# A single-core decode block: the last 256 rows of w2 by one indirect load of Pool's, and twelve rows to a partition

## The chip, the cores and the metric

The kernel runs on one core of one Trainium2 chip, and the core's five engines run side by side, each through its own list of instructions: TensorE (PE, with its weight loads shown as PEld), VectorE (DVE), ScalarE (ACT), GpSimd (POOL) and SyncE (SP), which here only issues transfers. Sixteen DMA engines carry out the transfers that SP, ACT and POOL issue.

The metric is the device time of one launch in microseconds (us). Before the change it is 391.63 us, the median of three runs (391.55 to 391.79). One more execution was recorded by the profiler; its own time is 391.81 us, and its recorded span, from the first instruction to the last, is 390.0 us.

## The reference

One decode step of a transformer block for 8 sequences, one token each, width D = 512. A condition vector gives six modulation vectors. Attention has 32 query heads and 8 key/value heads of width 128 over the last W = 2048 positions of a cache. A dense layer with F = 1792 hidden units and a squared ReLU follows.

```python
mod = (_silu(c) @ w_mod).reshape(8, 6, 1, -1)
sa, ca, ga, sb, cb, gb = (mod[:, i] for i in range(6))
h = _layernorm(x) * (1 + ca) + sa
q = (h @ wq).reshape(B, 1, 32, 128).transpose(0, 2, 1, 3)
k, v = (jnp.repeat(t[:, :, Sk - W:, :], 4, axis=1) for t in (k_cache, v_cache))
p = _softmax(jnp.einsum("bhqd,bhkd->bhqk", q, k) * 128 ** -0.5)
x = x + ga * (merge(jnp.einsum("bhqk,bhkd->bhqd", p, v)) @ wo)
h = _layernorm(x) * (1 + cb) + sb
r = jnp.maximum(h @ w1 + b1, 0)
x = x + gb * ((r * r) @ w2 + b2)
```

All of it is in float32. Nearly all the bytes are the cache: 8 sequences times 16.8 MB of K and V, beside w_mod (6.3 MB), wq and wo (8.4 MB each), w1 and w2 (3.7 MB each).

## The kernel before, in words

**Staging.** Four buffers of 4 MB, `slots`, hold whatever was loaded from DRAM. The list `loads` has the order: w_mod in two halves, wq in two halves, then for each sequence b two K loads and two V loads of 4 MB (the V loads one sequence behind), then wo in two halves, w1 and w2. `pump` issues the next loads on SP's queue as long as a slot is free, and `done` gives a slot back and calls `pump`. So a load can be issued only when the work on an earlier slot's content is over. The instruction list is written out by hand in this order; no scheduler moves anything.

**Completion semaphores.** A transfer of SP's or ACT's signals its landing on one of eight semaphores (DMAHW0 to DMAHW7 in the instruction lists). They are dealt out in rotation, in the order in which the transfers of both queues stand in the program. A transfer that is dealt a semaphore for the second time waits, in its issuing engine's list, until the earlier transfer on that semaphore has landed. Transfers that POOL issues have semaphores of their own (DMASW).

**Start.** Before the first `pump()` the program issues the small inputs: four transfers of `xc` (the token and condition rows) and `b1_in` on ACT (L63, L67), `b1_x` and `b2_in` on POOL (L68, L69). Then DVE and ACT make the SiLU of c, PE multiplies with w_mod (L238), DVE normalises, and PE multiplies with wq (L260).

**Each sequence.** DVE transposes K in place, in 32 by 32 blocks (`turn`, L307), PE multiplies with the queries (`scores`, L317), DVE and ACT make the softmax, and PE multiplies with V (`weighted`, L400) and collects the heads (`gather`).

**The dense layer, which the change rewrites.** w2 has 1792 rows, 14 to each of 128 partitions. Thirteen to a partition (FC = 13) come in five pieces into the last slot (L109 to L114): 4, 4, 3, 1 and 1 rows. The remaining 128 rows (`EXTRA`) go, four to a partition, to 20 and 12 partitions of `w2x`, which is the memory of `qb_all` used again; the two transfers stand on SP's queue behind w1 and ahead of the pieces of w2 (L106 to L108). POOL has zeroed the 64 partitions before (L325). The hidden units of the thirteen rows are computed by L517 and L520 in `ph`, those of the last 128 by L527 and L529 in `px`. ACT takes the ReLU of both (L542, L545), and DVE squares and transposes them (L551 to L555). The product with w2 runs in two parts. The first four rows of a partition and `w2x` go through a 512-wide accumulator (L562), which DVE and ACT copy out (L566, L567) and four matmuls fold in (L579). All other rows, 4 to 12, are multiplied by L572 straight into `py`, in the order in which their pieces land. L585, L586 and the store L587 end the program.

Of the kernel before, what the change touches and what calls it, by code (L numbers as in the profile page):

```python
# [18 lines left out]
def tile_adaln_cached_attention_mlp(  # L19
# [24 lines left out]
    FC = F // P - 1  # L44
# [19 lines left out]
    b1_in = consts.tile([NQ, FG], F32, name="b1_in")  # L64
# [3 lines left out]
    nc.gpsimd.dma_start(b1_x, b1[P * FC :].rearrange("(g n) -> g n", g=1))  # L68
# [12 lines left out]
    def load(key):  # L81
# [121 lines left out]
    rep = consts.tile([P, 4, 4, 32], F32, name="rep")  # L203
# [20 lines left out]
    rx = consts.tile([64, 32, 4], F32, name="rx")  # L224
# [84 lines left out]
    def scores(b, t):  # L309
# [14 lines left out]
        if b == B - 1 and t == 1:  # L324
            nc.gpsimd.memset(w2x[:64, :], 0.0)  # L325
# [184 lines left out]
    h2d = work.tile([P, NQ, 2, 32], F32, name="h2d", tag="prd", bufs=4)  # L510
    nc.vector.tensor_copy(h2d, h2T[:, :, None, :].to_broadcast([P, NQ, 2, 32]))
# [15 lines left out]
    nc.tensor.matmul(px[:64, :FX], one[:1, :1].to_broadcast([1, 64]), b1_x, start=True, stop=False)  # L527
    for kc in range(NQ):
        nc.tensor.matmul(  # L529
            px[:64, :FX],  # L530
            h2d[:, kc].rearrange("p a b -> p (a b)"),
            w1t[:, kc, P * FC :],
            start=False,
            stop=(kc == NQ - 1),
        )
    r = work.tile([P, 32, FC], F32, name="relu", tag="a")
    rT = work.tile([P, FC, 32], F32, name="rT", bufs=1)
    rxT = work.tile([64, 4, 32], F32, name="rxT", bufs=1)
    h = ph[:, :FG].rearrange("p (l c) -> p l c", l=32)
    halves = ((0, 6), (6, FC))  # L540
    for lo, hi in halves:
        nc.scalar.activation(r[:, :, lo:hi], h[:, :, lo:hi], AF.Relu)  # L542

    for g, o, _, at_ in EXTRA:
        nc.scalar.activation(  # L545
            rx[g : g + 32, : 4 * o, :].rearrange("p (o i) c -> p i o c", i=4),
            px[g : g + 32, at_ : at_ + 16 * o].rearrange("p (i o c) -> p i o c", i=4, o=o),
            AF.Relu,
        )
    for lo, hi in halves:  # L550
        nc.vector.tensor_mul(r[:, :, lo:hi], r[:, :, lo:hi], r[:, :, lo:hi])  # L551
        nc.vector.transpose(rT[:, lo:hi], r[:, :, lo:hi].rearrange("p l c -> p c l"))
        if lo == 0:
            nc.vector.tensor_mul(rx, rx, rx)
            nc.vector.transpose(rxT, rx.rearrange("p l c -> p c l"))  # L555

# [3 lines left out]
    chunks += [(rxT[:, c, :], w2x[:64, D * c : D * c + D]) for c in range(4)]  # L560
# [63 lines left out]
```

## Time and profile before

| | |
|---|---|
| median of three runs | 391.63 us |
| the profiled execution: its own time, its span | 391.81 us, 390.0 us |
| PE busy | 257.2 us, 66% of the span |
| DVE busy | 215.7 us, 55% |
| ACT, POOL busy | 42.8 us and 6.6 us |
| moved by DMA | 165.05 MB, mean 423 GB/s |
| on SP's queue | 7096 packets, 164.70 MB, 98.4% of the 16 DMA engines' time |
| mean granted TensorE clock | 0.836 of full speed |

The profile's page gives busy time by engine, the span in 40 slices, the chain of work that ended last, and the costliest groups of instructions. A timeline row has the start in us, the duration in us, the engine, the source line (L114 is line 114), the operation, the tile written and the tiles read, the shapes, a count, and in brackets the idle time of the engine ahead of it with what ended it. A name that ends in "q" (SPq) is the engine's sequencer. PE, PEld, DVE and ACT rows that follow each other are merged, so "x8" is eight records; a float32 matmul shows as two records. In the rows by window the last three numbers are the granted TensorE clock, the mean busy share of the 16 DMA engines and GB/s; packets are counted whole where they start.

### The profile page before, as it was taken

What the parts mean: (1) busy time and instruction counts of PE and PEld (TensorE: products, weight loads), DVE (VectorE), ACT (ScalarE), POOL (GpSimd) and SP (SyncE); (2) the same over time, 40 slices, a digit from 0 to 9 for tenths busy, and PEclk for the clock granted to TensorE, in tenths of its full rate; (3) what the DMA queues carried; (4) which work ended last, traced back from release to release, by engine and by line L of the source; (5) the groups of instructions that cost most, each with busy time, mean ns of one, the idle gap of its engine ahead of it and who ended that gap; (6) DMA issues with size and microseconds to landing.
All of it is one profiled execution on the core that took longest, in us unless ns stands there. A gap on an engine that the chain in (4) does not pass through costs nothing.

```text
span 390.0 us, 4820 instructions
## 1 busy us (share of the span) xinstructions
PE 257.2 (66%) x2126; PEld 111.1 (28%) x2126; DVE 215.7 (55%) x234; ACT 42.8 (11%) x91; POOL 6.6 (2%) x14
## 2 busy tenths in 40 slices
PE   0272808678975694859485938394749475985975
PEld 0120201151351343124322422233223313452332
DVE  3420199399394939293928391939292938330032
ACT  0310100030030003000300020003000300032010
POOL 4000000000000000000000000000000000100000
PEclk9998758969975986889778987797688779888889
DMA  8999999999999999999999999999999999999995
GB/s 325 432 434 428 430 430 434 434 444 439 435 437 428 427 432 434 430 428 430 429 430 428 434 430 432 437 439 430 439 434 434 426 437 425 434 435 413 424 421 207
DMA packets 7253, 165.05 MB, mean 423 GB/s; under 512 B 888, under 2 KB 1056, under 8 KB 1696
## 3 DMA queue, kind: packets, MB, share of 16 engines
q1 hardware_dynamic: 7096, 164.70, 98.4%
q8 instruction: 17, 0.28, 0.3%
q10 hardware_dynamic: 72, 0.04, 0.0%
q14 instruction: 4, 0.03, 0.0%
q0 software_dynamic: 64, 0.00, 0.0%
HBM read 164.67 MB, written 0.07 MB: 422 GB/s over the span
## 4 chain that ended last, share of the span: by engine, by line
DMA 53%; DVE 25%; PE 20%; ACT 1%; issue 1%; DVEq 0%; ACTq 0%; SPq 0%
DMA slot<-in_A_k_cache_dram 34%; DVE slot L307 22%; PE s_ps L317 16%; DMA slot<-in_B_w_dram 9%; DMA slot<-in_A_wq_dram 7%; DMA slot<-in_w_mod_dram 3%; PE t_ps L260 2%; PE t_ps L388 1%; PE o_ps L400 1%; PE m_ps L276 1%; DVE pT L389 0%; ACT prd L378 0%; DVE s L331 0%; DVE s L335 0%; DVE mx L340 0%
## 5 line engine op out<-in xcount | busy, mean ns | idle before, releaser
L307 DVE STREAM_TRANSPOSE slot<-slot 128x2048 f32<-128x2048 f32 x64 | 143.9, 2284 | 41.7 <-DMA slot<-in_A_k_cache_dram 41.7
L317 PE MATMUL s_ps<-slot,qb_all 128*32 128x512 f32 x512 | 121.7, 1099 | 68.4 <-DVE slot L307 67.5
L317 PEld LDWEIGHTS s_ps<-slot,qb_all 128*32 128x32 f32 x512 | 22.3, 136 | 147.7 <-issue 82.1
L400 PE MATMUL o_ps<-slot,pT 128*32 128x256 f32 x1024 | 59.7, 382 | 0.0
L400 PEld LDWEIGHTS o_ps<-slot,pT 128*32 128x32 f32 x1024 | 46.0, 112 | 27.7 <-issue 18.8
L388 PE MATMUL t_ps<-ident,prd 128*128 128x128 f32 x128 | 27.1, 373 | 16.5 <-ACT prd L378 9.5
L331 DVE STREAM_TRANSPOSE s<-s_ps 128x512 f32<-128x512 f32 x8 | 5.7, 717 | 54.2 <-PE s_ps L317 54.2
L388 PEld LDWEIGHTS t_ps<-ident,prd 128*128 128x128 f32 x128 | 20.2, 189 | 22.3 <-ACT prd L378 21.8
L378 ACT ACTIVATE prd<-pr,rz 128x512 f32<-128x512 f32 x32 | 20.5, 710 | 9.4 <-DVE rz L370 9.4
L354 ACT ACTIVATE pr<-s,nm 128x512 f32<-128x512 f32 x8 | 5.8, 722 | 141.2 <-DVE nm L348 141.2
L389 DVE TENSOR_TENSOR pT<-t_ps,m 128x512 f32<-128x512 f32 x32 | 20.4, 670 | 1.3 <-PE t_ps L388 1.2
L410 ACT COPY o_sb<-o_ps 128x256 f32<-128x256 f32 x16 | 5.8, 363 | 122.1 <-PE o_ps L400 122.1
L260 PE MATMUL t_ps<-slot,h1T 128*32 128x512 f32 x64 | 9.8, 764 | 8.9 <-DMA slot<-in_A_wq_dram 6.9
L475 PE MATMUL s_ps<-slot,oT 128*32 128x512 f32 x56 | 8.5, 773 | 4.5 <-DMA slot<-in_A_wo_dram 4.5
L173 PE MATMUL m_ps<-xsum,sel 128*128 128x1 f32 x2 | 0.6, 362 | 16.5 <-DVE xsum L196 16.5
L294 DVE TENSOR_TENSOR qb_all<-qrep,block 128x512 f32<-128x512 f32 x8 | 9.0, 1124 | 3.0 <-ACT qrep L286 3.0
L272 DVE STREAM_TRANSPOSE qT<-t_ps 128x512 f32<-128x512 f32 x2 | 1.4, 717 | 15.9 <-PE t_ps L260 15.7
L366 PE MATMUL m_ps<-z,same 128*128 128x1 f32 x16 | 3.3, 273 | 9.5 <-ACT pr L354 9.5
L238 PE MATMUL m_ps<-slot,cT 128*32 128x384 f32 x64 | 7.8, 658 | 0.0
L325 POOL MEMSET qb_all<- 64x2048 f32 x1 | 1.8, 1807 | 331.9 <-PE s_ps L317 331.9
L489 DVE COPY at_i<-s_ps 128x256 f32<-128x256 f32 x1 | 0.4, 425 | 12.2 <-PE s_ps L475 12.2
L260 PEld LDWEIGHTS t_ps<-slot,h1T 128*32 128x32 f32 x64 | 2.4, 133 | 16.1 <-DMA slot<-in_A_wq_dram 7.8
(113 smaller groups left out, 102.5 us busy)
## 6 DMA issues: line engine op xcount, KB each, us to landing
slot<-in_A_k_cache_dram SPq DMA_DIRECT2D x16, 4096.0 KB, 18.6
slot<-in_A_v_cache_dram SPq DMA_DIRECT2D x16, 4096.0 KB, 28.2
slot<-in_A_wq_dram SPq DMA_DIRECT2D x2, 4096.0 KB, 26.4
slot<-in_w_mod_dram SPq DMA_DIRECT2D x2, 3072.0 KB, 17.2
slot<-in_A_wo_dram SPq DMA_DIRECT2D x1, 4096.0 KB
slot<-in_A_wo_dram SPq DMA_DIRECT2D x1, 2048.0 KB
slot<-in_A_wo_dram SPq DMA_DIRECT2D x2, 1024.0 KB
slot<-in_B_w_dram SPq DMA_DIRECT2D x2, 1024.0 KB
```

What stands on the lines that cost most here:

```text
L238: nc.tensor.matmul(pm[i][32 * q : 32 * q + 32, : 3 * P].rearrange("p (m n) -> p m n", m=3), cT[:, kc, :], wm[:, 3 * i : 3 * i + 3, q, :], ...
L260: nc.tensor.matmul(pq[t][32 * x : 32 * x + 32, :], hT[:, kc, :], w[:, 2048 * t + 512 * x : 2048 * t + 512 * x + 512], start=(kc == 0), sto ...
L294: nc.vector.tensor_mul(qb[b % 2][:, :, :, :REP], qrep_b[:, :, None, :, b].to_broadcast([P, 32, 4, REP]), block[:, None, :, None].to_broadc ...
L307: nc.vector.transpose(k, k)
L317: nc.tensor.matmul(S_[b][32 * x : 32 * x + 32, :].rearrange("p (j i) -> p j i", i=8), q[:, n : n + 32], k[:, :, c, :, x], start=(t == 0 an ...
L354: nc.scalar.activation(pr.rearrange("p j (a i) -> p j a i", a=4), S2_.pop(b).rearrange("p (a j i) -> p j a i", a=4, i=8), AF.Exp, bias=NM_ ...
L378: nc.scalar.activation(d, pr[:, 4 * n : 4 * n + 4, :, None].to_broadcast([P, 4, 32, 4]), AF.Copy, scale=RZ_[b][0])
L388: nc.tensor.transpose(pp[:, P * i : P * i + P], d[:, i].rearrange("p i u -> p (i u)"), one)
L389: nc.vector.tensor_mul(PT_[b][:, n].rearrange("p q j (x r) -> p q (j x) r", r=REP), pp.rearrange("p (y q r) -> p q y r", y=16, r=REP), m16 ...
L400: nc.tensor.matmul(o[32 * (m % 4) : 32 * (m % 4) + 32].rearrange("p u d -> p (u d)"), PT_[b][:, n, 2 * q + t, 2 * u : 2 * u + 2, :].rearra ...
L410: nc.scalar.copy(O_[b][:, t], o)
L475: nc.tensor.matmul(wo_ps[32 * (i % 4) : 32 * (i % 4) + 32, :], oT[:, i, :], slot(("wo", i // 16), D)[:, i % 16, :], start=(i < 4), stop=(i ...
```

## The change

FC becomes 12: twelve rows of w2 to a partition come by SP's queue, in pieces of 4, 4, 2, 1 and 1 rows. The last 256 rows, in 64 groups of four (8 KB), go to 64 of the 128 partitions of `w2x` by one indirect load of POOL's, L348. It reads a list of 128 group numbers, one for each partition; a number beyond the last group means that nothing is moved to this partition. `EXTRA` now lists the chosen partitions as (quarter, first lane, number of lanes, first group): all of partitions 0 to 20, 27 to 44, 48 to 51, 60 to 68, 92 to 99 and 124 to 127. The list is made at the start, by a memset and nine iotas on POOL (L233, L235), a transpose and a conversion on DVE (L243, L245). The load is issued behind the memset of `w2x` (now all 128 partitions), after the last scores. `b1_x` and `b2_in` move from POOL's queue to ACT's. The hidden units of the last rows are now 256: `px` is computed for 128 columns of output partitions and 256 values wide, its ReLU is split into four pieces on ACT and five on DVE, and DVE handles `rx` behind the second half of `r` rather than ahead of it.

```diff
-    FC = F // P - 1
+    FC = F // P - 2
...
-    nc.gpsimd.dma_start(b1_x, b1[P * FC :].rearrange("(g n) -> g n", g=1))
-    nc.gpsimd.dma_start(b2_in, b2.rearrange("(g n) -> g n", g=NQ))
-    EXTRA = ((0, 5, P * FC, 0), (32, 3, P * FC + 80, 80))
+    nc.scalar.dma_start(b1_x, b1[P * FC :].rearrange("(g n) -> g n", g=1))
+    nc.scalar.dma_start(b2_in, b2.rearrange("(g n) -> g n", g=NQ))
+    EXTRA = (
+        (0, 0, 21, 0), (0, 27, 5, 21), (1, 0, 13, 26), (1, 16, 4, 39), (1, 28, 4, 43),
+        (2, 0, 5, 47), (2, 28, 4, 52), (3, 0, 4, 56), (3, 28, 4, 60),
+    )
...
-            for g, o, first, _ in EXTRA:
-                v = w2[first : first + 16 * o].rearrange("(i o c) n -> o i (c n)", i=4, o=o)
-                nc.sync.dma_start(w2x[g : g + 4 * o, :], v)
-            cuts = ((0, 4), (4, 8), (8, 11), (11, 12), (12, 13))
+            cuts = ((0, 4), (4, 8), (8, 10), (10, 11), (11, 12))
...
+    place_r = work.tile([P, 32], F32, name="mt", bufs=1)
+    nc.gpsimd.memset(place_r, float(F))
+    for g, l, n, first in EXTRA:
+        nc.gpsimd.iota(place_r[32 * g : 32 * g + 1, l : l + n], pattern=[[1, n]],
+            base=P * FC // 4 + first, channel_multiplier=0, allow_small_or_imprecise_dtypes=True)
+    place_c = work.tile([P, 32], F32, name="nm")
+    nc.vector.transpose(place_c, place_r)
+    nc.vector.tensor_copy(places, place_c[:, 0:1])
...
-            nc.gpsimd.memset(w2x[:64, :], 0.0)
+            nc.gpsimd.memset(w2x, 0.0)
+            nc.gpsimd.indirect_dma_start(w2x, None, w2.rearrange("(r c) n -> r (c n)", c=4),
+                bass.IndirectOffsetOnAxis(ap=places[:, :1], axis=0),
+                bounds_check=F // 4 - 1, oob_is_err=False)
...
-    nc.tensor.matmul(px[:64, :FX], one[:1, :1].to_broadcast([1, 64]), b1_x, start=True, stop=False)
+    nc.tensor.matmul(px[:, :FX], one[:1, :1].to_broadcast([1, P]), b1_x, start=True, stop=False)
...
-    for g, o, _, at_ in EXTRA:
-        nc.scalar.activation(
-            rx[g : g + 32, : 4 * o, :].rearrange("p (o i) c -> p i o c", i=4),
-            px[g : g + 32, at_ : at_ + 16 * o].rearrange("p (i o c) -> p i o c", i=4, o=o), AF.Relu)
-    for lo, hi in halves:
+    for i, (g, l, n, first) in enumerate(EXTRA):
+        to = rx[32 * g : 32 * g + 32, l : l + n, :]
+        v = px[32 * g : 32 * g + 32, 4 * first : 4 * (first + n)].rearrange("p (l c) -> p l c", c=4)
+        if i % 2:
+            nc.scalar.activation(to, v, AF.Relu)
+        else:
+            late.append((to, v))
+    for n, (lo, hi) in enumerate(halves):
+        if n:
+            for to, v in late:
+                nc.vector.tensor_scalar(to, v, 0.0, None, op0=ALU.max)
         nc.vector.tensor_mul(r[:, :, lo:hi], r[:, :, lo:hi], r[:, :, lo:hi])
-        nc.vector.transpose(rT[:, lo:hi], r[:, :, lo:hi].rearrange("p l c -> p c l"))
-        if lo == 0:
+        if n:
             nc.vector.tensor_mul(rx, rx, rx)
             nc.vector.transpose(rxT, rx.rearrange("p l c -> p c l"))
+        nc.vector.transpose(rT[:, lo:hi], r[:, :, lo:hi].rearrange("p l c -> p c l"))
```

The change moves instructions and waits at three places. The first is the head of SP's list, the loads of w_mod (slots 88 and 89) and wq (slots 90 and 91). Before:

```order
L114 DMA slot_88<-in_w_mod_dram 128x6144
L114 DMA slot_89<-in_w_mod_dram 128x6144
L114 DMA slot_90<-in_A_wq_dram 128x8192
L114 DMA slot_91<-in_A_wq_dram 128x8192 [waits DMAHW0_49]
L91 DMA slot_88<-in_A_k_cache_dram 128x1x8192 [waits DMAHW1_49,PE_49]
```

and of the change:

```order
L121 DMA slot_88<-in_w_mod_dram 128x6144
L121 DMA slot_89<-in_w_mod_dram 128x6144 [waits DMAHW0_49]
L121 DMA slot_90<-in_A_wq_dram 128x8192 [waits DMAHW1_49]
L121 DMA slot_91<-in_A_wq_dram 128x8192 [waits DMAHW2_49]
L102 DMA slot_88<-in_A_k_cache_dram 128x1x8192 [waits DMAHW3_49,PE_49]
```

DMAHW0 is signalled by the first half of w_mod in both, DMAHW1 to DMAHW4 by the four transfers of `xc`, DMAHW5 by `b1_in`. With `b1_x` and `b2_in` on ACT's queue, DMAHW6 and DMAHW7 are theirs, and the rotation comes back to DMAHW0 at the second half of w_mod instead of at the second half of wq.

The second place is DVE's list behind the normalisation of the dense layer, from the copy of h2T on. Before:

```order
L511 COPY h2d<-h2T 128x256 [waits DVE_49]
L551 TENSOR_TENSOR relu<-relu 128x32x6 [waits Activation_49]
L552 STREAM_TRANSPOSE rT<-relu 128x192 [waits DVE_49]
L554 TENSOR_TENSOR rx<-rx 64x128 [waits Activation_49]
L555 STREAM_TRANSPOSE rxT<-rx 64x128 [waits DVE_49]
L551 TENSOR_TENSOR relu<-relu 128x32x7
L552 STREAM_TRANSPOSE rT<-relu 128x224 [waits DVE_49]
```

and of the change:

```order
L541 COPY h2d<-h2T 128x512 [waits DVE_49]
L586 TENSOR_TENSOR relu<-relu 128x32x6 [waits Activation_49]
L590 STREAM_TRANSPOSE rT<-relu 128x192 [waits DVE_49]
L585 TENSOR_SCALAR rx<-m_ps 32x84 [waits PE_49,Activation_49]
L585 TENSOR_SCALAR rx<-m_ps 32x52
L585 TENSOR_SCALAR rx<-m_ps 32x16 x3
L586 TENSOR_TENSOR relu<-relu 128x32x6
L588 TENSOR_TENSOR rx<-rx 128x128 [waits DVE_49]
L589 STREAM_TRANSPOSE rxT<-rx 128x128 [waits DVE_49]
L590 STREAM_TRANSPOSE rT<-relu 128x192
```

Five pieces of the ReLU come in ahead of the square of `rx`; the first of them waits for PE and for ACT, and the second half's square (L586) now stands ahead of `rx`.

The third is ACT's list at the same point: what is taken from `m_ps` (that is `px`) into `rx`. Before:

```order
L542 ACTIVATE relu<-t_ps 128x32x6 [waits PE_49]
L542 ACTIVATE relu<-t_ps 128x32x7
L545 ACTIVATE rx<-m_ps 32x4x5x4 [waits PE_49,Pool_49]
L545 ACTIVATE rx<-m_ps 32x4x3x4
L567 COPY at_y<-s_ps 128x256 [waits DVE_49,Activation_49]
```

and of the change:

```order
L573 ACTIVATE relu<-t_ps 128x32x6 [waits PE_49]
L573 ACTIVATE relu<-t_ps 128x32x6
L579 ACTIVATE rx<-m_ps 32x20 [waits PE_49,Pool_49]
L579 ACTIVATE rx<-m_ps 32x16
L579 ACTIVATE rx<-m_ps 32x20
L579 ACTIVATE rx<-m_ps 32x16
L602 COPY at_y<-s_ps 128x256 [waits DVE_49,Activation_49]
```

Two pieces became four. ACT counts its semaphore up once, behind the fourth, and it is this count that DVE's first L585 waits for.

More of the change, by code (lines that the diff above doesn't have):

```diff
@@ L199, in tile_adaln_cached_attention_mlp @@
     nc.scalar.activation(warm, eps, AF.Exp)
-    rep = consts.tile([P, 4, 4, 32], F32, name="rep")
+    rep = work.tile([P, 4, 4, 32], F32, name="rep", tag="prd", bufs=4)
     nc.vector.tensor_copy(
@@ L223, in tile_adaln_cached_attention_mlp @@
         nc.gpsimd.memset(t, 0.0)
-    rx = consts.tile([64, 32, 4], F32, name="rx")
+    place_r = work.tile([P, 32], F32, name="mt", bufs=1)
+    nc.gpsimd.memset(place_r, float(F))
+    for g, l, n, first in EXTRA:
+        nc.gpsimd.iota(
+            place_r[32 * g : 32 * g + 1, l : l + n],
+            pattern=[[1, n]],
+            base=P * FC // 4 + first,
+            channel_multiplier=0,
+            allow_small_or_imprecise_dtypes=True,
+        )
+    place_c = work.tile([P, 32], F32, name="nm")
+    nc.vector.transpose(place_c, place_r)
+    places = consts.tile([P, 1], mybir.dt.uint32, name="places")
+    nc.vector.tensor_copy(places, place_c[:, 0:1])
+    rx = consts.tile([P, 32, 4], F32, name="rx")
     nc.gpsimd.memset(rx, 0.0)
@@ L324, in scores @@
         if b == B - 1 and t == 1:
-            nc.gpsimd.memset(w2x[:64, :], 0.0)
+            nc.gpsimd.memset(w2x, 0.0)
+            nc.gpsimd.indirect_dma_start(
+                w2x,
+                None,
+                w2.rearrange("(r c) n -> r (c n)", c=4),
+                bass.IndirectOffsetOnAxis(ap=places[:, :1], axis=0),
+                bounds_check=F // 4 - 1,
+                oob_is_err=False,
+            )
         done(("K", b, t))
@@ L509, in tile_adaln_cached_attention_mlp @@
     h2T = scaled(xm, rstd, mods[1][:, 0, :], "h2T")
-    h2d = work.tile([P, NQ, 2, 32], F32, name="h2d", tag="prd", bufs=4)
-    nc.vector.tensor_copy(h2d, h2T[:, :, None, :].to_broadcast([P, NQ, 2, 32]))
+    h2d = work.tile([P, NQ, 4, 32], F32, name="h2d", tag="prd", bufs=4)
+    nc.vector.tensor_copy(h2d, h2T[:, :, None, :].to_broadcast([P, NQ, 4, 32]))
     w1t = slot(("w1",), F)
```

21 lines of the change are left out of this document (14 added, 7 removed).

## The prediction

> **What bounds the kernel now.** I read the page's slices first, then the queue's landings and the chain that ended last, then the two ends of the program by window and timeline.
>
> ```profile
> GB/s 325 432 434 428 430 430 434 434 444 439 435 437 428 427 432 434 430 428 430 429 430 428 434 430 432 437 439 430 439 434 434 426 437 425 434 435 413 424 421 207
> slot<-in_A_k_cache_dram SPq DMA_DIRECT2D x16, 4096.0 KB, 18.6
> ```
>
> Between the first slice and the last the transfers move about 432 GB/s in every slice, whatever the engines do. A K load is 4.19 MB and takes 9.7 us at that rate, but lands 18.6 us after its issue: each load is issued behind some 7 to 9 us of earlier work. The queue does not run dry in the middle, so the stream of bytes is the bound. Idle time put into the stream cannot be made up later, and an engine that is faster in the middle gains nothing. What is left to win or lose lies at the ends, so I took these from the chain:
>
> ```profile
> 0.74 10.36 DMA slot<-in_w_mod_dram
> 11.11 27.54 DMA slot<-in_A_wq_dram
> 45.67 2.01 PE m_ps L276 x8
> 47.71 0.78 ACT qrep L286 x4
> ...
> 376.05 10.34 DMA slot<-in_B_w_dram
> 386.39 0.04 issue
> 386.43 0.47 PE t_ps L572 x8
> ```
>
> The last piece of w2 releases the last eight matmul records at 386.43; two DVE steps and the store follow. At the start the first half of w_mod has landed at 11.10, and this landing is something that SP waits for:
>
> ```profile
> SPq L114 <- DMA slot<-in_w_mod_dram: 9.0, 1, 9.0
> ...
> ACT L161 <- DMA xc_in<-in_xc_dram: 12.6, 1, 12.6
> ...
> 0.74 0.86 SPq L114 DMA_DIRECT2D slot<-in_w_mod_dram  x2
> 1.64 9.80 SPq L114 DMA_DIRECT2D slot<-in_A_wq_dram  x2
> ```
>
> By the order of SP's list it is the fourth load (the second half of wq) that waits here. It costs nothing now: the second half of w_mod and the first half of wq (7.3 MB) are queued before the wait begins.
>
> **The change, term a: the start.** With two more transfers on ACT's queue the semaphore of the first load comes round at the second load. So the same landing now holds the second half of w_mod, with nothing queued behind the first but small inputs. The stream stops and starts again. How long a start takes is shown at the program's head:
>
> ```profile
> 1.25:1.50 0.25, 0.00 (x0) 0.00 (x0) 0.00 (x0) 0.00 (x0) 0.25 (x1) 1.00 0.00 0
> 1.50:2.00 0.50, 0.00 (x0) 0.00 (x0) 0.00 (x0) 0.00 (x0) 0.50 (x2) 1.00 2.64 590
> 2.00:2.50 0.50, 0.00 (x0) 0.00 (x0) 0.00 (x0) 0.00 (x0) 0.50 (x2) 1.00 0.60 147
> 2.50:3.00 0.50, 0.00 (x0) 0.00 (x0) 0.00 (x0) 0.00 (x0) 0.42 (x3) 1.00 0.19 49
> 3.00:3.50 0.50, 0.00 (x0) 0.00 (x0) 0.45 (x2) 0.00 (x0) 0.50 (x1) 1.00 0.46 197
> 3.50:4.00 0.50, 0.00 (x0) 0.00 (x0) 0.50 (x1) 0.00 (x0) 0.50 (x2) 1.00 0.93 393
> ```
>
> Issued at 0.74, nothing flows up to 1.5; by 4.0 the half microseconds add up to 688 KB. At 430 GB/s from the issue on it would be 3.26 x 430 = 1402 KB. The lost 714 KB are 1.66 us: the price of a start, from issue to full rate. The least that term a can cost is this, if an engine works on the first load up to its landing. The most follows from when the work runs out. The load is 3146 KB, and by the same windows 3244 KB have been started by 10.0, so its last packets start at 9.8 on average; the stream is back at 11.11 + 1.66 = 12.8, 3.0 us later. An engine that is late at the landing loses less than the mean, and it is late ones that end the program. I take **2.3 us**, between 1.7 and 3.0. Nothing behind refills it: the loads that follow on SP each wait for an `xc` transfer, which has landed by 12.6 (ACT's first wait), under the 7.3 us of the second half of w_mod.
>
> The Trainium skill, DMA: Bandwidth & Descriptors, section Anatomy of one DMA, gives a fixed cost of about 2.0 us to a transfer, most of it the receipt of the last byte, on the path that Pool issues. Taken as the gap, it is an estimate of 2.0 for this term and 0.3 less for the sum; the windows above, from SP's queue, show 1.66 without the receipt.
>
> **Term b: the dense layer's chain.** It hangs on the landing of the last piece of w1:
>
> ```profile
> 378.17 0.18 PEld L520 LDWEIGHTS t_ps<-slot,h2T 128*32 128x32 f32 x8 [1.21 <-DMA slot<-in_B_w_dram]
> 379.03 0.43 PE L527 MATMUL m_ps<-b_x,ident 1*64 1x128 f32 x2
> 379.39 1.09 PE L529 MATMUL m_ps<-slot,h2d 128*64 128x128 f32 x8
> 380.57 0.44 ACT L545 ACTIVATE rx<-m_ps 32x80 f32<-32x80 f32 x2 [0.80 <-PE m_ps L529]
> 381.05 0.28 DVE L554 TENSOR_TENSOR rx<-rx 64x128 f32<-64x128 f32 x1 [0.58 <-ACT rx L545]
> 381.36 0.41 DVE L555 STREAM_TRANSPOSE rxT<-rx 64x128 f32<-64x128 f32 x1
> 381.70 0.34 DVE L551 TENSOR_TENSOR relu<-relu 128x224 f32<-128x224 f32 x1
> 381.96 1.06 PE L562 MATMUL s_ps<-qb_all,rxT 64*32 64x512 f32 x8
> 384.26 0.40 PE L579 MATMUL t_ps<-at_y,sel 128*32 128x128 f32 x8
> 385.15 1.08 PE L572 MATMUL t_ps<-slot,rT 128*32 128x128 f32 x32 [0.49 <-DMA slot<-in_B_w_dram]
> ```
>
> Today `px` is done at 380.48, `rxT` feeds PE at 381.96, and PE is through with L579 at 384.66. From there five rows' matmuls remain; four cost 1.08, so without waits PE would end at 384.66 + 1.35 = 386.01. It ends at 386.90, because the pieces of w2 come later. So this chain has 0.9 us of cover. Now the steps of the change:
>
> - PE: `px` is 256 wide instead of 128. L276 is the same shape of matmul (128 by 128 weights, 256 columns): four take 2.01, against 1.09. With the bias row's second half (0.2) and 0.07 less for L520's 384 columns, +1.05. Lower bound 0, if width were free; upper +1.5, twice L527 and L529.
> - ACT: four pieces instead of two. L286 gives 0.195 for a small copy out of PSUM: 0.78 against 0.44, +0.35 (0 to 0.5).
> - DVE: its five pieces stand behind ACT's fourth by the semaphore, not beside it. The 128x32 step L346 takes 0.18, and five at that spacing or a little closer are 0.75 (0.4 to 1.0). Ahead of the square of `rx` now also stands L586 for the second half, 0.32 by L551's row. Together +1.07.
>
> ```profile
> 340.56 0.18 DVE L346 TENSOR_SCALAR mb<-mq 128x32 f32<-128x32 f32 x1
> ```
>
> The sum is 2.5 us: `rxT` reaches PE at 384.45 instead of 381.96. From there to L579's end PE needs 2.70 as today, and the four remaining rows 1.08: it ends at 388.25 instead of 386.90. One row less to multiply is in this. Term b is **+1.4**. With all lower bounds (0, 0 and 0.72) the chain ends at 386.5 (-0.4), with all upper ones (1.5, 0.5 and 1.3) at 389.0 (+2.1).
>
> **Term c: the moved bytes.** The total is the same: 256 KB in `w2x` and thirteen rows, or 512 KB and twelve. POOL is free to issue at 339.7:
>
> ```profile
> 337.85 1.81 POOL L325 MEMSET qb_all<- 64x2048 f32 x1 [331.91 <-PE s_ps L317]
> 5.78 0.16 POOL L229 MEMSET mx<- 128x32 f32 x1
> 1.24 0.65 POOL L68 DMA_DIRECT2D b_x<-in_B_b_dram  x1 [0.80 <-POOLq L610]
> ```
>
> Its 512 KB now share the engines with V and wo, ahead of w1, and could hold back w1's landing, where term b begins, by up to 524 KB / 430 = 1.2 us. It is less as far as the chosen partitions lie with DMA engines that are ahead, and that some are ahead shows at the end:
>
> ```profile
> 383.00:384.00 1.00, 1.00 (x30) 0.88 (x30) 0.42 (x1) 0.38 (x1) 0.00 (x0) 1.00 0.78 324
> 384.00:385.00 1.00, 0.67 (x26) 0.40 (x16) 0.00 (x0) 0.00 (x0) 0.00 (x0) 1.00 0.78 305
> 385.00:386.00 1.00, 0.85 (x32) 0.77 (x32) 0.00 (x0) 0.00 (x0) 0.00 (x0) 1.00 0.44 170
> 386.00:387.00 1.00, 0.66 (x19) 0.16 (x8) 0.07 (x1) 0.00 (x0) 0.00 (x0) 1.00 0.09 18
> ```
>
> A fifth of the engines' time is idle from 383 on, more than half from 385. I take **+0.2**, between 0 and 1.2. The gain at the end of w2 (below) is real, but PE comes later by term b, so I count it as nothing.
>
> **What costs nothing.** The memset of all 128 partitions has the same 2048 elements in each. The indirect load itself has no row here; nothing stands behind it on POOL, and between 339.7 and 384 it has 44 us for 512 KB, against 1.2 us of bytes at full rate and 6.5 us of issue even at ten times L68's 0.65. The nine iotas cost from 1.4 us (nine times L229's 0.16) up to what is free: POOL is done at 5.9, and DVE's work ahead of L248 ends 6.27 us before 25.57, at 19.3; that leaves 13 us, and DVE idles behind it. ACT's two further issues lie in its wait for `xc`.
>
> ```profile
> 25.57 0.56 DVE L248 COPY mod<-m_ps 128x384 f32<-128x384 f32 x1 [6.27 <-PE m_ps L238]
> ```
>
> **The sum.** 2.3 + 1.4 + 0.2 = 3.9 us. The profiled execution took 391.81, so 395.7; the median was 0.18 lower, so 395.5.
>
> **The rivals.**
> 1. *Balance wins.* The end of w2 is uneven: 817 KB are moved from 383 on, which all sixteen engines would do in 1.9 us, ending about 1.1 us before the 386.0 at which the bytes end now. If the 64 partitions are the right ones, if term b stays inside its 0.9 us of cover and if the gap at the start is absorbed by a queue that has slack after all, the end comes by about 0.9 sooner: 390.7. For it speak the idle shares above. Against it, the steady 432 GB/s and the 18.6 us landings, which leave nowhere to absorb 2 us; it decides only if term a is under about 0.9, below its lower bound. By the rule in the Trainium skill, DMA: Bandwidth & Descriptors, section The descriptor swizzle (four neighbouring partitions to an engine), the chosen partitions put 64 KB on seven engines, 40 KB on one and 8 KB or nothing on eight; I work out an estimate of 0.6 us from 16 KB less on these. No row here tells the engines apart.
> 2. *The gap alone.* If the longer chain of the dense layer is hidden by a later end of w2, or its pieces overlap more than I think, only the start costs: 391.63 + 2.2 = 393.8.
> 3. *More is late.* If the indirect load moves slowly between other queues' packets and lands behind 384, or holds back w1 by the full 1.2 us, L562 waits for it: 397 or more.
> 4. *It cancels.* A gap at 1.7 whose loss is half regained, and a balanced end: within 0.2% of before, 391.6.
>
> **How the numbers follow.** The forecast (all three terms) has 0.62, rival 2 0.17, rival 3 0.10, rival 1 0.07, rival 4 0.04. The range takes the bounds of a (-0.6, +0.7) and most of those of b, and reaches rival 2: 393.0 to 397.2. A measurement of this kernel tells about 0.2% (0.8 us) from no change. Slower by more than that: forecast, rivals 2 and 3, 0.89. Within: 0.04. Faster: 0.07.
>
> **What would show it.** Term a: SP's second load issued near 11 and a hole in GB/s between 10 and 13, with everything behind later by about 2.3, the second wq landing near 41. Term b: `px` two microseconds long, L585 behind L579, the last L607 without a wait for a transfer. Term c: L550's wait for w1 unchanged, L597 without a wait for the indirect load. I am wrong if the second load's issue is early, or if the hole is there and K's first landing is not later.

## The result, and the profile after

| | before | after |
|---|---|---|
| median (range) of six runs each (before: the three known already and three more) | 391.63 us (391.55 to 391.79) | 396.38 us (396.10 to 398.02) |
| profiled execution: own time, span | 391.81 us, 390.0 us | 396.44 us, 394.7 us |

The ratio is 1.0128 (95% interval 1.0111 to 1.0145): the change makes the kernel slower by 1.28%, 4.75 us by the medians and 4.63 us by the profiled executions. The prediction was 395.5 us, within 393.0 to 397.2.

The first two fences are the start of the kernel after the change: SP's loads by the timeline (start, duration, queue, line, operation), and the windows (PE, PEld, DVE, ACT and POOL busy, then TensorE's granted clock, the share of the DMA engines, GB/s).

```profile
0.74 10.46 SPq L121 DMA_DIRECT2D slot<-in_w_mod_dram  x2
11.26 0.90 SPq L121 DMA_DIRECT2D slot<-in_A_wq_dram  x2
```

```profile
8.00:9.00 1.00, 0.00 (x0) 0.00 (x0) 0.00 (x0) 0.00 (x0) 0.00 (x0) 1.00 0.92 395
9.00:10.00 1.00, 0.00 (x0) 0.00 (x0) 0.00 (x0) 0.00 (x0) 0.00 (x0) 1.00 0.79 333
10.00:11.00 1.00, 0.00 (x0) 0.00 (x0) 0.00 (x0) 0.00 (x0) 0.00 (x0) 1.00 0.05 11
11.00:12.00 1.00, 0.00 (x0) 0.00 (x0) 0.00 (x0) 0.69 (x1) 0.00 (x0) 1.00 1.05 246
12.00:13.00 1.00, 0.00 (x0) 0.00 (x0) 0.06 (x1) 0.90 (x2) 0.00 (x0) 1.00 0.65 147
13.00:14.00 1.00, 0.00 (x0) 0.00 (x0) 0.97 (x2) 0.00 (x0) 0.00 (x0) 1.00 0.68 295
14.00:15.00 1.00, 0.00 (x0) 0.00 (x0) 0.93 (x4) 0.00 (x0) 0.00 (x0) 1.00 0.93 393
```

The first row merges both loads of w_mod: the issue of the second one is not over until 11.2, where before it was the second half of wq that ended at 11.44. From 10 to 11 the stream stands still, and it is at full rate again only behind 14. Whether it is made up later is told by two wide windows, of before and then of after:

```profile
0.00:16.00 16.00, 0.00 (x0) 0.00 (x0) 4.71 (x9) 1.59 (x2) 4.82 (x13) 1.00 0.92 370
16.00:376.00 360.00, 247.49 (x1998) 106.82 (x2002) 207.59 (x217) 39.83 (x84) 1.81 (x1) 0.83 1.00 431
```

```profile
0.00:16.00 16.00, 0.59 (x2) 0.50 (x2) 4.54 (x12) 1.63 (x3) 4.68 (x21) 1.00 0.77 296
16.00:376.00 360.00, 244.37 (x1980) 110.38 (x1980) 206.26 (x212) 39.50 (x83) 2.95 (x2) 0.82 1.00 432
```

In the first 16 us 74 GB/s are missing, which is 1.18 MB or 2.75 us at 430 GB/s. In the 360 us behind them the rate is the same to 1 GB/s, and the last K load that DVE waits for still lands 2.8 us later (321.13 before, 323.92 after). The loss stays.

At the end the timeline of after reads:

```profile
381.34 0.20 PEld L550 LDWEIGHTS t_ps<-slot,h2T 128*32 128x32 f32 x8 [1.48 <-DMA slot<-in_B_w_dram]
383.06 1.99 PE L559 MATMUL m_ps<-slot,h2d 128*128 128x256 f32 x8
385.15 0.74 ACT L579 ACTIVATE rx<-m_ps 32x20 f32<-32x20 f32 x4 [2.01 <-PE m_ps L559]
385.92 0.91 DVE L585 TENSOR_SCALAR rx<-m_ps 32x84 f32<-32x84 f32 x5 [2.05 <-ACT rx L579]
386.87 0.36 DVE L586 TENSOR_TENSOR relu<-relu 128x192 f32<-128x192 f32 x1
387.92 1.06 PE L597 MATMUL s_ps<-qb_all,rxT 128*32 128x512 f32 x8 [1.87 <-DVE rxT L589]
390.45 1.06 PE L607 MATMUL t_ps<-slot,rT 128*32 128x128 f32 x32
391.57 0.29 DVE L620 TENSOR_TENSOR y<-t_ps,mod 128x128 f32<-128x128 f32 x1 [2.09 <-PE t_ps L607]
```

The last piece of w1 lands at 381.34 instead of 378.17, 3.17 us later. From there PE's last row took 8.73 us before (to 386.90, held up by w2's pieces); now PE ends at 391.51, 10.17 us behind the landing, with no wait for a transfer in the chain's last steps. So 3.17 + 1.44 = 4.61 us, against 4.63 in the execution's own time. (Some 0.3 of the 1.44 is a lower clock and not the longer chain; the second experiment shows it.) What w2 gained lies unused: its bytes have ended by 388, 3.5 us ahead of PE.

### The profile page after: what moved, and what is told of

Its sections match the earlier page's. It is cut to its first block, busy times and chain, and to the rows that moved or that the text cites. A ratio compares the mean times of both kernels' runs of the same rounds, so it can differ in the third digit from the quotient of the medians.

```text
span 394.7 us, 4820 instructions
## 1 busy us (share of the span) xinstructions
PE 257.8 (65%) x2118; PEld 116.7 (30%) x2118; DVE 216.4 (55%) x241; ACT 43.0 (11%) x93; POOL 7.6 (2%) x23
## 4 chain that ended last, share of the span: by engine, by line
DMA 51%; DVE 25%; PE 21%; issue 1%; ACT 1%; SPq 0%; ACTq 0%; DVEq 0%
DMA slot<-in_A_k_cache_dram 33%; DVE slot L329 22%; PE s_ps L339 15%; DMA slot<-in_A_wq_dram 8%; DMA slot<-in_B_w_dram 7%; DMA slot<-in_w_mod_dram 3%; PE t_ps L282 2%; PE t_ps L418 1%; PE o_ps L430 1%; DVE pT L419 1%; PE m_ps L298 1%; PE m_ps L559 0%; PE t_ps L607 0%; ACT prd L408 0%; DVE s L361 0%
## 5 line engine op out<-in xcount | busy, mean ns | idle before, releaser
L339 PEld LDWEIGHTS s_ps<-slot,qb_all 128*32 128x32 f32 x512 | 23.3, 136 | 145.6 <-issue 80.4
L430 PEld LDWEIGHTS o_ps<-slot,pT 128*32 128x32 f32 x1024 | 50.1, 112 | 24.0 <-issue 18.0
L282 PE MATMUL t_ps<-slot,h1T 128*32 128x512 f32 x64 | 11.5, 887 | 12.8 <-DMA slot<-in_A_wq_dram 12.8
L347 POOL MEMSET qb_all<- 128x2048 f32 x1 | 1.8, 1804 | 335.0 <-PE s_ps L339 335.0
L260 PE MATMUL m_ps<-slot,cT 128*32 128x384 f32 x64 | 6.9, 596 | 0.0
```

The costliest lines, as they stand in the source:

```text
L260: nc.tensor.matmul(pm[i][32 * q : 32 * q + 32, : 3 * P].rearrange("p (m n) -> p m n", m=3), cT[:, kc, :], wm[:, 3 * i : 3 * i + 3, q, :], ...
L282: nc.tensor.matmul(pq[t][32 * x : 32 * x + 32, :], hT[:, kc, :], w[:, 2048 * t + 512 * x : 2048 * t + 512 * x + 512], start=(kc == 0), sto ...
L339: nc.tensor.matmul(S_[b][32 * x : 32 * x + 32, :].rearrange("p (j i) -> p j i", i=8), q[:, n : n + 32], k[:, :, c, :, x], start=(t == 0 an ...
L430: nc.tensor.matmul(o[32 * (m % 4) : 32 * (m % 4) + 32].rearrange("p u d -> p (u d)"), PT_[b][:, n, 2 * q + t, 2 * u : 2 * u + 2, :].rearra ...
```

## The experiments

All times are medians with their range, beside runs of the kernel before on the same chip (391.57 or 391.64 us in these groups). Three questions were asked: is the gap at the start the whole of the 3.2 us, what do the chosen partitions do, and what in the chain of the dense layer can be had back. In the code cuts, "..." stands for arguments or lines left out.

**The gap alone**, in the kernel before:

```diff
-    nc.gpsimd.dma_start(b1_x, ...)
-    nc.gpsimd.dma_start(b2_in, ...)
+    nc.scalar.dma_start(b1_x, ...)
+    nc.scalar.dma_start(b2_in, ...)
```

> The kernel before with b1_x and b2_in issued on ACT's queue, nothing else changed. Theory (the second load of w_mod waits for the first, the stream stops once, nothing makes it up): second load issued near 11.2, second wq landed near 41.8 instead of 38.7, last piece of w2 near 389.5 instead of 386.4, time 391.63 + 3.1 = 394.7. Rival (the moved issues are harmless, and the 4.7 us of the change come from the indirect load and the dense layer): 391.6 within 0.5.

Measured: 394.84 us (394.49 to 394.90), ratio 1.008 (1.0063 to 1.0096), +3.27 us. Its windows at the start show the same hole, with nothing else changed:

```profile
9.00:10.00 1.00, 0.00 (x0) 0.00 (x0) 0.00 (x0) 0.00 (x0) 0.00 (x0) 1.00 0.67 282
10.00:11.00 1.00, 0.00 (x0) 0.00 (x0) 0.00 (x0) 0.00 (x0) 0.00 (x0) 1.00 0.05 13
11.00:12.00 1.00, 0.00 (x0) 0.00 (x0) 0.00 (x0) 0.53 (x1) 0.00 (x0) 1.00 0.19 49
12.00:13.00 1.00, 0.00 (x0) 0.00 (x0) 0.00 (x0) 0.99 (x2) 0.00 (x0) 1.00 1.32 319
```

and by its chain of waits the second half of wq lands at 41.90, against 38.65 before:

```profile
0.73 10.28 DMA slot<-in_w_mod_dram
11.88 30.02 DMA slot<-in_A_wq_dram
```

At the end this kernel still waits for w2, whose last piece lands at 389.28 instead of 386.43, 2.85 us later:

```profile
389.28 0.16 PEld L572 LDWEIGHTS t_ps<-slot,rT 128*32 128x32 f32 x8 [0.41 <-DMA slot<-in_B_w_dram]
```

Two small inputs on another queue, far from the bound by their size, cost about two thirds of the whole change: 3.27 of 4.75 us by the medians, 3.00 of 4.63 by the profiled executions.

**The change without the gap**: the change with both inputs left on POOL.

```diff
-    nc.scalar.dma_start(b1_x, ...)
-    nc.scalar.dma_start(b2_in, ...)
+    nc.gpsimd.dma_start(b1_x, ...)
+    nc.gpsimd.dma_start(b2_in, ...)
```

> The changed kernel with b1_x and b2_in back on POOL's queue. Theory: second wq lands at 38.7 as before, last piece of w1 near 378.2, the dense layer's chain from there 10.2 us long as in the changed kernel, PE's end near 388.4, time 391.63 + 1.45 = 393.1. If part of the 3.2 us of w1's delay is the moved 512 KB (term c), w1 lands later than 378.2 by that part. Rival (start is harmless): 396.4 as the changed kernel.

Measured: 394.10 us (393.52, 393.59, 394.60, 395.40), ratio 1.0074 (1.0052 to 1.0096). In the profiled run (393.52) the second half of wq lands at 38.74 and w1's last piece at 378.61, 0.44 us later than before; from there PE needs 9.84 us, 1.11 more than the 8.73 before. These two make 1.55 of the 1.7 us by which its span is longer. The fastest two runs are 0.4 to 0.5 above the 393.1 that was expected; the median lies higher, by a spread that the kernel before does not have (391.41 to 391.87).

The 9.84 us are 0.33 less than the change's 10.17. The difference lies in the last quarter of `ph`, right behind w1's landing: from there to PE's next row it takes 1.10 us in the change (381.34 to 382.44) and 0.78 here (378.61 to 379.39), and the granted clock is 0.50 there and 1.00 here. The two windows, of the change and then of this kernel:

```profile
380.00:382.00 2.00, 1.83 (x14) 0.20 (x8) 0.00 (x0) 0.00 (x0) 0.00 (x0) 0.50 1.00 413
```

```profile
378.00:380.00 2.00, 1.70 (x14) 0.45 (x10) 0.11 (x1) 0.47 (x2) 0.00 (x0) 1.00 0.99 414
```

The windows of its end:

```profile
384.00:385.00 1.00, 0.13 (x4) 0.13 (x8) 0.96 (x4) 0.00 (x0) 0.00 (x0) 1.00 0.82 315
385.00:386.00 1.00, 1.00 (x9) 0.16 (x6) 0.21 (x1) 0.00 (x0) 0.00 (x0) 1.00 0.08 29
```

The bytes of w2 all but stop at 385, where before 170 GB/s still moved from 385 to 386: the end is better balanced by about 1 us. The chain ends at 388.45 in this run, so nothing comes of it.

With this run there are four kernels, with and without the gap and with and without the rest of the change. These are landings by their profiles, in us:

| landing | before | gap alone | change without the gap | change |
|---|---|---|---|---|
| second half of wq | 38.65 | 41.90 | 38.74 | 41.86 |
| last K load that DVE waits for | 321.13 | 324.18 | 320.86 | 323.92 |
| last piece of w1 | 378.17 | 381.29 | 378.61 | 381.34 |

The gap moves them by 3.05 to 3.25 us in the kernel before and by 2.73 to 3.12 in the change. By the times of the profiled executions the gap alone costs 3.00 us and the rest alone 1.71, together 4.71, against 4.63 for the whole change: the two parts add up.

**One transfer on ACT**, the other on POOL, to tell whether every moved transfer costs something or only the place at which the rotation comes round:

```diff
-    nc.scalar.dma_start(b2_in, ...)
+    nc.gpsimd.dma_start(b2_in, ...)
```

> The changed kernel with b1_x on ACT's queue and b2_in on POOL's. Theory (the rotation of the eight semaphores): DMAHW0 now comes round at the first half of wq, which waits with the second half of w_mod already queued (7.3 us of work), so no gap: as the kernel with both on POOL, 393.1 within 0.4. Rival (each further small transfer on ACT's queue disturbs the start by itself): half way, about 394.7.

Measured: 395.24 us (393.35, 393.36, 395.22, 395.26, 395.82, 396.12), ratio 1.0076 (1.0054 to 1.0099). By the median one would say half the gap. The profile says otherwise: now the first half of wq waits for the first landing (issued at 11.60), with w_mod's second half queued behind the first; w1's last piece lands at 379.03, 2.3 us ahead of the change's. The two runs near 393.35 are at the fastest of the kernel without a gap (393.52), as the rotation has it; neither has a profile. In the profiled run (396.12) PE ends 2.58 us later than in the profile without a gap: 0.42 us lie at w1's landing, 0.55 between the landing and `rxT`, and 1.61 behind `rxT`. In these last two stretches the granted clock is at 0.50 for a time; the second is shown here:

```profile
384.00:386.00 2.00, 0.16 (x4) 0.16 (x8) 1.89 (x9) 0.00 (x0) 0.00 (x0) 1.00 0.56 215
386.00:388.00 2.00, 2.00 (x22) 0.91 (x18) 0.61 (x2) 0.37 (x1) 0.00 (x0) 0.75 0.00 0
388.00:390.00 2.00, 2.00 (x48) 1.84 (x44) 0.00 (x0) 0.00 (x0) 0.00 (x0) 0.50 0.00 0
390.00:392.00 2.00, 1.03 (x28) 0.73 (x20) 0.58 (x2) 0.00 (x0) 0.00 (x0) 0.89 0.00 0
```

Four rows of w2 take 1.94 us here, from 387.42 on, against 1.08 at a granted clock of 1.00 in the profile of the change. This kernel's median cannot speak on the rotation; its landings can.

**Other partitions**: the change without the gap, with the 64 partitions that the change leaves out, as nearly as whole groups allow.

```diff
-        (0, 0, 21, 0), (0, 27, 5, 21), (1, 0, 13, 26), ...
+        (0, 20, 8, 0), (1, 20, 8, 8), (2, 4, 24, 16), (3, 4, 24, 40),
```

> As the changed kernel with both small inputs on POOL, but the 64 partitions are others: 20 to 27 and 52 to 59, 68 to 91 and 100 to 123, in four runs instead of nine (so two pieces of the ReLU on ACT and two on DVE: the chain of the dense layer is about 0.9 us shorter). Theory (four neighbouring partitions to a DMA engine, and these engines are the ones that are late): no balance, the late engines have 64 KB more before w1 and 48 KB more in all; the last piece of w1 lands up to 2 us later than in the kernel with the chosen partitions, and the bytes of w2 end near 387.9 instead of 385.0. Rival (any 64 partitions do the same, or the load is spread over all engines anyway): w1 within 0.3 of the kernel with the chosen partitions, bytes end at the same time, total 0.9 less by the shorter chain.

Measured: 394.88 us (394.70, 395.06), ratio 1.0083 (1.0063 to 1.0103). The windows of its end:

```profile
384.00:385.00 1.00, 1.00 (x9) 0.16 (x8) 0.28 (x2) 0.43 (x2) 0.00 (x0) 1.00 0.47 197
385.00:386.00 1.00, 0.12 (x4) 0.00 (x0) 0.94 (x4) 0.00 (x0) 0.00 (x0) 1.00 0.50 205
386.00:387.00 1.00, 0.77 (x8) 0.16 (x8) 0.58 (x2) 0.00 (x0) 0.00 (x0) 1.00 0.52 201
387.00:388.00 1.00, 1.00 (x19) 0.65 (x19) 0.42 (x1) 0.12 (x1) 0.00 (x0) 1.00 0.18 70
```

Half of the engines' time is idle for three microseconds, and by the windows the bytes end some 2.2 us later than with the change's partitions; w1's last piece lands 2.1 us later (380.73). Its faster run is 1.2 us behind the fastest with the change's partitions, although its chain from w1's landing to PE's end is shorter (9.09 us against 9.84). So it matters which partitions take the 512 KB, and of these two choices the change's is the better one. The profiles do not tell the DMA engines apart. The Trainium skill, DMA: Bandwidth & Descriptors, section The descriptor swizzle, gives four neighbouring partitions to an engine; by that rule these 64 partitions load eight engines and leave eight nearly free, which agrees with the shares of 0.47 to 0.52.

**An earlier `px`**: the change without the gap, in which the bias row of `px` stands ahead of all `ph` matmuls, and the `px` matmul of each quarter of the contraction over D ahead of that quarter's `ph` matmuls, so that little of `px` is left behind w1's landing.

```diff
+    nc.tensor.matmul(px[:, :FX], one[:1, :1].to_broadcast([1, P]), b1_x, ...)
     for kc in range(NQ):
+        nc.tensor.matmul(px[:, :FX], h2d[:, kc]..., w1t[:, kc, P * FC :], ...)
         for g in range(NQ):
             nc.tensor.matmul(ph[32 * g : 32 * g + 32, :FG], ...)
```

> The changed kernel with b1_x and b2_in on POOL (no gap), and PE's list altered in one place: the bias row of px and the px matmul of each quarter of w1 stand ahead of that quarter's four ph matmuls, so that only a quarter of px is behind w1's last landing. Theory (term b's first step is the width of px on the chain): the chain from w1's landing to PE's end is about 2 us shorter (8.2 instead of 10.2), the time 391.6 to 391.9 where the kernel without a gap had 393.5 in its fastest runs. Theory on the spread (the runs of 395 and more are those in which the granted clock of TensorE falls to 0.5 in the last 4 us, which a chain that ends before about 387 escapes): spread under 0.7 us. Rival (px lies beside ACT and DVE anyway, the pieces on these set the end): no more than 0.5 saved. Rival on the spread (the indirect load's landing varies): it stays 2 us.

Measured: 397.07 us (396.24 to 397.39), ratio 1.0131 (1.0116 to 1.0146): 3 us slower, not faster. The windows of its end:

```profile
374.00:376.00 2.00, 1.44 (x5) 0.64 (x3) 0.99 (x3) 0.00 (x0) 0.00 (x0) 0.79 1.02 427
376.00:378.00 2.00, 2.00 (x10) 0.52 (x10) 0.00 (x0) 0.00 (x0) 0.00 (x0) 0.50 1.02 424
378.00:380.00 2.00, 2.00 (x12) 0.64 (x11) 0.00 (x0) 0.00 (x0) 0.00 (x0) 0.86 1.02 426
...
386.00:392.00 6.00, 6.00 (x82) 3.85 (x74) 0.45 (x2) 0.37 (x1) 0.00 (x0) 0.50 0.01 3
```

The stretch ahead of w1's landing was not free. PE is busy without a break from 376 to 382, part of it at half clock, and its rows no longer wait for w1's last piece: its own work has become the bound. `rxT` reaches PE at 385.68, 0.8 us later than in the profile without a gap (384.87). The larger part of the loss lies behind it: here PE is at half clock again through the whole tail, 386 to 392, and needs 6.66 us from `rxT` to its end instead of 3.58. Whether the early `px` brings this on is not shown.

**A shorter tail on top of it**: all nine ReLU pieces of `px` on ACT, and DVE takes the ReLU and the square of `ph`, so that no engine waits for the other's pieces; and the same rearrangement, with the early `px`, in the kernel before.

```diff
-    for lo, hi in halves:
-        nc.scalar.activation(r[:, :, lo:hi], h[:, :, lo:hi], AF.Relu)
...
+    for g, l, n, first in EXTRA:
+        nc.scalar.activation(rx[32 * g : 32 * g + 32, l : l + n, :], ..., AF.Relu)
...
+        nc.vector.tensor_scalar(r[:, :, lo:hi], h[:, :, lo:hi], 0.0, None, op0=ALU.max)
```

> As f1_px_early, and the ReLU is divided otherwise: all nine pieces of px on ACT, both halves of ph on DVE (a maximum, then the square), so that no DVE step waits for ACT's pieces but the square of rx. Theory (steps two and three of term b are DVE waiting behind ACT): another 0.5 to 0.9 off the chain, which then ends at or before the last piece of w2; with the bytes of w2 ending 1.2 us earlier than before by the chosen partitions, PE ends near 386.1 and the time is 390.8, below both kernels. Rival (the chosen partitions bring nothing once the chain is short, because the last landing is as late as before): 391.6.

> The kernel before (thirteen rows, no indirect load) with the same two alterations of the dense layer. Theory (its end is the landing of w2's last piece, the chain has 0.9 us of cover): no gain, 391.6 within 0.3. Rival (the shorter chain is the gain of f3_new_tail, not the balance): as much faster as f3_new_tail, about 390.8.

Measured: 393.92 us (393.34 to 395.49), ratio 1.006 (1.0045 to 1.0075), and in the kernel before 393.01 us (392.37 to 393.50), ratio 1.0035 (1.0022 to 1.0048). Both miss what was expected. In the first PE is busy from 376 to beyond 382, as in the experiment just shown. Counted from the first `px` matmul behind the bias row, `rxT` reaches PE 9.57 us later instead of 10.56, so in these two profiles the new division wins 1.0 us. Most of what lies between the two times is the clock: from `rxT` to PE's end it is 3.56 us here, at full clock, against 6.66. The kernel before loses 1.4 us by the same edits; how much of it is the early `px` and how much the new division between ACT and DVE was not told apart.

**`px` by quarters**: the change without the gap, where each group of 32 partitions computes only its own values (32 partitions by 104, 84, 36 and 32 columns) instead of all 256 on 128 partitions.

```diff
-    nc.tensor.matmul(px[:, :FX], h2d[:, kc]..., w1t[:, kc, P * FC :], ...)
+    for g in range(NQ):
+        nc.tensor.matmul(px[32 * g : 32 * g + 32, 4 * lo[g] : 4 * hi[g]], h2T[:, kc, :],
+            w1t[:, kc, P * FC + 4 * lo[g] : P * FC + 4 * hi[g]], ...)
```

> The changed kernel with b1_x and b2_in on POOL (no gap), in which each quarter of px is computed only for the columns that its lanes use: four matmuls of 32 output partitions and 104, 84, 36 and 32 columns in place of one of 128 by 256, in the old place behind ph. Theory (step one of term b, the width of px, is 1.0 us of the chain): L559's 1.99 us become about 1.0, and the chain from w1's landing to PE's end 9.1 instead of 10.2; fastest runs 392.4 to 392.6 where they were 393.4. Rival (px is not on the chain, since ACT and DVE end later anyway): 393.4. On the spread: as PE ends about 1 us earlier, fewer runs reach the phase of half clock, but some may.

Measured: 393.29 us (392.38 to 394.16), ratio 1.0039 (1.0025 to 1.0053). The fastest run is 1.1 us under the fastest of the change without the gap, and `px` takes about 0.9 us instead of 1.99 (the row has 31 of its 32 records):

```profile
380.92 0.81 PE L550 MATMUL m_ps<-slot,h2T 128*32 128x104 f32 x31
```

From the start of `px` to `rxT` it is 3.82 us instead of 4.86. The profiled run itself (393.38) shows no gain at its end, since ahead of `px`, at half clock, it took 2.36 us from w1's landing instead of 1.40. So the width of `px` was a cost that could be had back: 1.0 to 1.1 of the 2.0 us by which the chain is longer without the gap (9.84 us, against the 7.84 that PE would have needed before if it had not waited for w2).

**Quarters, the shorter tail, and `px` behind `ph`**: the kernel just shown, with nine pieces on ACT and `ph` on DVE, the bias row ahead, and in the contraction over D the first three quarters of `px` behind their `ph` and only the last ahead of it.

```diff
+        if kc == NQ - 1:
+            extra(kc)
         for g in range(NQ):
             nc.tensor.matmul(ph[32 * g : 32 * g + 32, :FG], ...)
+        if kc < NQ - 1:
+            extra(kc)
```

> As g2_px_quarters, with the bias row of px ahead of all, the first three quarters of w1 multiplied into px behind ph of the same quarter, the last one ahead of ph; all nine pieces of the ReLU on ACT, both halves of ph on DVE. PE's added work before w1's last landing is 0.75 us at full clock, 1.5 at half, against 1.0 to 1.5 us of idle there (f1_px_early put 2.1 to 4 us there and PE became the bound). Theory: the chain from w1's landing to PE's end is 7.5 to 8 us, PE ends near 386.3, the time is 390.9 to 391.2 in its fastest runs, below the kernel before. Rival (any work added in that stretch meets the half clock and moves the end by as much): 392 or more.

Measured, in eleven runs: 391.43 us (391.23 to 392.53), ratio 0.9999 (0.9990 to 1.0008). That is 5 us under the change, 2.3 of it (by the medians) from leaving the two inputs on POOL, and the same as before. Its end, by the timeline, hangs on w2 again:

```profile
386.00 0.16 PEld L606 LDWEIGHTS t_ps<-slot,rT 128*32 128x32 f32 x8 [0.39 <-DMA slot<-in_B_w_dram]
386.50 0.29 DVE L619 TENSOR_TENSOR y<-t_ps,mod 128x128 f32<-128x128 f32 x1 [2.42 <-PE t_ps L606]
```

The last piece releases PE at 386.00 instead of 386.43: this is what the balanced end is worth at a landing, in this one profile. The fastest runs would show it, the spread takes it back; a gain over before is not shown.

**All pieces on ACT**: the change without the gap, with no piece on DVE.

```diff
-        if i % 2:
-            nc.scalar.activation(to, v, AF.Relu)
-        else:
-            late.append((to, v))
+        nc.scalar.activation(to, v, AF.Relu)
```

> The changed kernel with b1_x and b2_in on POOL (no gap) and all nine pieces of px's ReLU on ACT, none on DVE. Theory (step three of term b: DVE's five pieces wait for ACT's fourth, and the square of the second half stands behind them): the nine pieces take 1.16 us on ACT, as in f3_new_tail, in place of 0.74 and then 0.91; the second half's square (0.3) runs beside them; the chain from w1's landing to PE's end is 9.4 instead of 10.2, the fastest runs 392.7 instead of 393.4. Rival (the pieces overlap by half anyway, or nine on one engine cost as much): 10.0 to 10.2.

Measured: 393.28 us (392.69 to 393.63), ratio 1.0038 (1.0023 to 1.0052). The timeline of its tail:

```profile
381.89 1.16 ACT L578 ACTIVATE rx<-m_ps 32x84 f32<-32x84 f32 x9 [2.02 <-PE m_ps L559]
383.08 0.29 DVE L585 TENSOR_TENSOR rx<-rx 128x128 f32<-128x128 f32 x1 [2.25 <-ACT rx L578]
```

Nine pieces in a row on ACT take 1.16 us; four on ACT and five on DVE took 0.74 + 0.91, one behind the other. From w1's landing to PE's end it is 9.06 us instead of 9.84. Splitting the pieces over two engines cost 0.8 us: 0.5 because DVE waited for ACT's count, so that they did not run side by side, and 0.3 because the square of the second half of `r` then stood behind them instead of being done while ACT worked.

## Why the prediction was right, and where it was off

- **Term a, the start: the mechanism was right, the size was too small.** The rotation, the second load behind the first landing, the hole between 10 and 13 and the later K loads are all there, and taking the two inputs away from ACT takes them away. The term was put at 2.3 us, within 1.7 to 3.0. By the mean of the stream it measured 2.75 us in the change and 2.94 in the kernel with the gap alone (370 - 291 GB/s over 16 us); the landings moved by 2.7 to 3.3 us, w2's last one by 2.85, and the time by 3.00 in the profiled executions and 3.27 by the medians. The step that failed is "An engine that is late at the landing loses less than the mean": the landings lost as much as the mean. The upper bound was taken from the mean as well, and many landings pass it. Whether they truly move 0.1 to 0.3 us more than the stream is not settled; no run told the DMA engines apart at the start.
- **Term b, the chain: right in its mechanism, and nearer in its sum than in its parts.** +1.4 was predicted, and +1.44 measured in the change, but +1.11 without the gap, where the last quarter of `ph` had the full clock. By the steps: `px` 1.99 for 2.0, ACT's four pieces 0.74 for 0.78, DVE's five 0.91 for 0.75. `rxT` reached PE 6.58 us behind w1's landing (6.26 without the gap) where 6.28 was forecast, and from there PE needed 3.59 where 3.78 was. That the sum came out to 0.1 is in part luck: the half clock added 0.3, and the tail was 0.2 shorter. PE did not wait for w2 in its last rows, and the chain of waits ended with w1. What made the sum come near at all was that the cover of 0.9 us was taken off first. Of the 2.0 us by which the chain is longer without the gap, a narrower `px` gives back 1.1 and one engine for all pieces 0.8, by their fastest runs.
- **Term c, the moved bytes: within its bounds.** 0.2 us was taken. The landings of two profiles differ by up to 0.7 us even ahead of the indirect load, so w1's last piece is best counted from the last K load: it comes 0.7 us later without the gap than before, and 0.3 later in the change than with the gap alone and with one input on ACT than before. One profile of each does not tell these from 0.2.
- **What was to cost nothing cost nothing.** POOL issued the indirect load at 342.66, it landed 17.3 us later, and it was wanted at 387.9. The nine iotas were done at 4.4.
- **Rival 1, the balance**, is real as a mechanism: about 1 us at the end of w2's bytes, 0.43 us at the last landing where the chain allows it. It lost for the reasons that were given, the lengthened chain and the gap ahead of it. **Rival 2, the gap alone,** would have given 393.8 (with 2.2 us for the start, where the term has 2.3); the gap alone gives 394.84, and the change is 1.5 us above that. **Rival 3** needed a late indirect load, which there was not. **Rival 4** needed the gap's loss to come back, and the rate behind 16 us and the landings in the table exclude that.

The sum was 3.9 us for 4.6 measured: terms a and c together are 0.7 too small (2.5 for the 3.17 by which w1 landed later), and term b is right to 0.1, with the help of the clock.

## What to carry to other kernels

Before a small transfer goes to another queue, count the transfers against the completion semaphores that they share: one more or less decides which large load waits, and where transfers are the bound, as here, a gap at the start is still there at the end. A chain behind the last loads has only the cover that the transfers still to come give it; measure that cover first, and shorten the chain (narrower matmuls, one engine for all the small pieces) before bytes are balanced. An engine that looks idle ahead of a landing is no free place for work if its clock is at half speed there.

## What the hardware showed that was not expected

- A stream of loads that is let run dry for one landing loses 2.75 to 2.94 us of stream and 2.7 to 3.1 us at w1's landing, some 370 us later.
- TensorE's granted clock falls to 0.50 for a stretch while it is working: in all twelve profiles once between 373 and 382, and in two of them (one input on ACT, the early `px`) again between 385 and 393. Followed in windows of 0.25 us, these stretches have only two lengths, 3.4 us and 6.8 us, and in the two profiles with two of them the second starts 10.2 us, three times 3.4, behind the first: the clock seems to be set anew every 3.4 us. In the run with one input on ACT this took four rows of w2 from 1.08 to 1.94 us.
- Kernels that end with PE's own chain (those of four or more runs) spread over 0.9 to 2.8 us from run to run. Of those that wait for w2 at the end, the kernel before spreads over 0.7 at most, in the group with most runs, and the one with the gap alone over 0.4; but the one with `px` by quarters and the shorter tail, which waits so in its profile, spreads over 1.3. The two profiles with a second low stretch suggest that the clock makes the wider spread; it is not shown, since each kernel has only one profile.
- In the run with one input on ACT the second low stretch comes a microsecond behind 1.87 us of idle PE (383.97 to 385.84). The Trainium skill, TensorE: Matmul & The Clock Gate, section What's actually happening, puts the clock down to how busy PE was in a window that runs free of the program. That agrees with the fixed lengths. But the change has the same 1.87 us of idle at the same place of its list, from 386.05 to 387.92, and keeps the full clock behind it, as its two windows show; what sets off the low stretch is not shown here.

```profile
386.00:388.00 2.00, 0.13 (x8) 0.08 (x8) 1.89 (x9) 0.00 (x0) 0.00 (x0) 1.00 0.75 293
388.00:390.00 2.00, 2.00 (x34) 1.04 (x38) 0.69 (x2) 0.37 (x1) 0.00 (x0) 1.00 0.02 8
```

- The indirect load moves only the chosen rows: 512 KB for 64 of 128 indices, in 144 packets, at 1.15 us of POOL's time and 17.3 us to its landing amid a full stream.
- In three runs the time is 2.8 to 2.9 us over the span, in the others 1.7 to 2.2: the change without the gap has 394.60 us with a span of 391.7, the same span as its profiled run of 393.52. Part of the spread thus lies outside the span; what it is stays open.
